# A fused attention and Mish block on one core: the weighted sums of two steps in one block, ScalarE's other work every second step

## The chip, the cores and the metric

The kernel runs on one core of one Trainium2 chip. The metric is the device time in microseconds, the median of several runs. A profile of one execution, taken by the hardware profiler, goes with it. The core's engines run side by side: TensorE (PE; its weight loads are listed as PEld), VectorE (DVE), ScalarE (ACT), GpSimd (POOL), and SyncE (SP), which issues the DMAs here. Results of matmuls land in PSUM, eight banks of 128 partitions by 512 words of 32 bits.

## What is computed

```python
x = A_x                                   # 1 x 2048 x 512
xn = _layernorm(x, axis=-1)
s = _A_ref(xn, A_wq, A_wk, A_wv, A_wo)    # attention, 32 query heads of 16, one k and v head
g = _silu(_B_ref(xn, B_w1, B_b1, B_w2))   # 512 -> 1792, Mish, 1792 -> 512
return x + s * g
```

In A, scores are q k / 4, softmax runs over all 2048 keys, and the heads' outputs are multiplied by wo. In B, the activation is h * tanh(softplus(h)).

## The kernel before

**The work in steps.** Queries are taken in NU = 32 units: 512 tokens (one of four token chunks) by four heads. Each unit goes through the 2048 keys in 16 steps of 128 keys, so there are NS = 512 steps; the main loop runs them in order at s = 0, 1, 2, ... A step holds four kinds of matmul on TensorE:

- **e** (e_one, L1098): four score matmuls of 64 contraction rows, 128 keys by 512 queries. ScalarE turns each into a pt tile with Exp (L1100). Even and odd steps use different halves of the array's rows; two steps together make two key blocks.
- **m** (m_one, L1119): score matmuls of a later unit, the other way round, of which VectorE takes the maximum (L1123); it is subtracted later. Mostly four a step.
- **xps**: a part of a "group", the other dense work (query projections, the two layers of the MLP, the wo product). A group has 12 or 15 matmuls in FP32R, high and low parts of each operand (mm12). Mm.half (L120) runs each as two halves of 64 rows, both into one PSUM bank.
- **pv** (pv, L1187): the weighted sums. For each key block, four matmuls with 128 rows and 32 output columns, one in each quarter of the columns; pt is FP32 here, and each stands as two instructions in the trace, so a step has eight. They accumulate over a unit's 16 steps in one bank.

e, m and xps use one half of the rows each, so two of them run at a time, one on each half; pv uses all rows.

**The banks.** Three for e, three for m, one for pv, one for xps.

**How a step is written down.** `waves(h, em, new)` issues the row matmuls of a step, h = s % 2. If no chunk is open it may take a new one, when `new` allows that and a group is ready: part of a group, mostly 6 of 12 matmuls, or 8 and then 7 of 15 (`chunk_size`). In this step it issues the chunk's first halves, in rows h, alternating with e and m matmuls on the other rows; in the next step the second halves, in the rows of the other h. Because both halves write one bank, the first matmul of a half is made to wait for a **relay**: the exponential or maximum of the e or m matmul that waves issued just behind the last xps matmul of the half before. The lines:

```python
i = xs.popleft().half(ps, h)
if first and cur["relay"] is not None:
    tc.add_manual_dep(i.ins, cur["relay"].ins.name, ...)
...
if len(a) > 1 or a and not xs:
    r = a.popleft()()
    if k and not xs and relay is None:
        relay = r
```

After the last chunk of a group, finish runs its `post`, which evacuates the bank with ScalarE or VectorE. `em` gives the order of e and m ("MEMEMEME"), m_sides how many m go on each half.

**The order around it.** After waves come `act_jobs` (ScalarE's other work: the Exp and Ln of the Mish, of the gate, and of the softmax sums, kept in the queue `jobs`, each of which starts the next piece of its own chain, on POOL too), `due` (what is timed for this step: DMAs and POOL work) and `pv_to(s - 2)`, which issues pv of the steps up to s - 2. When a unit's 16 are done, pv_to calls o_out: a copy of the bank on ScalarE (os), eight DMAs on SP, and later the two jobs of the softmax sums. `gap` counts evacuations on ScalarE, and act_jobs gives out less when there was one. Ready times and due times are kept in planned steps (STEP_US = 2.95), at build time; the order on every engine is fixed. The last LEAD = 20 steps (from s = 492) run two at a time through late_pair, with pv_to at every second one; a scheduled stage ahead of the loop does the loading, layernorm, keys and values and the first query projections.

Of the kernel before, what the change touches and what calls it, by code (L numbers as in the profile page):

```python
# [33 lines left out]
LEAD = 20  # L34
# [28 lines left out]
def m_need(v):  # L63

    return (34, 64)[v] if v < 2 else 32 * (v + 1)
# [61 lines left out]
def block_kernel(ctx: ExitStack, tc: tile.TileContext, x, wq, wk, wv, wo, w1, b1, w2, out):  # L127
# [275 lines left out]
    jobs = deque()  # L403
# [5 lines left out]
    gap = [0]  # L409
    ran = [0]  # L410

    def act_jobs(n):
        n = (int(len(jobs) > 3) if gap[0] else n) if n < 9 else n
        gap[0] = 0
        while n > 0:
            k = next((k for k, (fn, free) in enumerate(jobs)
                      if free is None or free() is not None and free() <= step[0]), None)
            if k is None:
                return
            fn = jobs[k][0]  # L420
            del jobs[k]
            fn()
            n -= 1
            ran[0] += 1
# [128 lines left out]
    def begin():  # L553
        prepare()
        if qqueue and is_ready(qqueue[0]):
            g = qqueue.popleft()
        elif queue and is_ready(queue[0]):
            g = queue.popleft()
        else:
            n = next((n for n, g in enumerate(queue) if g.wo is None), None)  # L560
            if not n or not is_ready(queue[n]) or queue[n].m1 is None:
                return False
            g = queue[n]
            del queue[n]
        if g.start:
            g.start()
        if len(g.mms) == 15 and spare_steps() > 1:
            g.most = 5
        if g.alloc:
            ps = g.alloc()  # L570
        else:
            ps = ps_x.tile([P, 512], F32, tag="x", name="xps")
        cur.update(g=g, n=0, ps=ps, chunk=[], relay=None)
        return True

    def finish():
        g = cur["g"]
        if cur["n"] < len(g.mms):
            return False
        for i in g.items:  # L580
            i.users -= 1
        cur["g"] = None
        evacs[0] += g.dve
        if lead:
            lead["post"](g, cur["ps"])
        else:
            g.post(cur["ps"])
            g.done = step[0]
        return True
# [98 lines left out]
    def chunk_size(n, most):  # L688
        return -(-n // -(-n // most)) if n else 0

    def waves(h, em, new):

        if not cur["chunk"] and (not new or cur["g"] is None and not begin()):
            mms = []
        else:
            g = cur["g"]
            mms = cur["chunk"] or g.mms[cur["n"]:cur["n"] + chunk_size(len(g.mms) - cur["n"], g.most)]  # L700
        second = bool(cur["chunk"])
        k = len(mms)
        ms = em(k, second)
        a = deque(ms[1 - h])
        b = deque(ms[h])
        ps = cur["ps"]
        ends = second and cur["n"] + k == len(cur["g"].mms)
        xs = deque(mms)
        swap = k % 2 and k > 5 and not second
        relay = None  # L710
        first = True
        done = False
        while a or b or xs:
            if xs:
                i = xs.popleft().half(ps, h)
                if first and cur["relay"] is not None:
                    tc.add_manual_dep(i.ins, cur["relay"].ins.name, mybir.DependencyInfo(
                        mybir.DependencyClass.Sync, mybir.DependencyReason.DATA), reason="other half of the bank")
                first = False
                if ends and cur["g"].dve and len(xs) == HOLD + k % 2:  # L720
                    held[0] = []
                if not xs and ends:
                    cur["n"] += k
                    cur["chunk"] = []
                    finish()
                    done = True
                    for top in held[0] or ():
                        top()
                    held[0] = None
            elif b and not swap:  # L730
                b.popleft()()
# [4 lines that stand above are left out]
            if b and swap and not xs and not a:  # L736
                b.popleft()()
        if k and not done:
            assert relay is not None
            cur["relay"] = relay  # L740
            if second:
                cur["n"] += k
                cur["chunk"] = []
            else:
                cur["chunk"] = mms
# [432 lines left out]
    def pv(s):  # L1178
        v, k = divmod(s, 16)
        if k == 0:  # L1180
            pv_of[v] = ps_v.tile([P, C], F32, tag="v", name=f"pv{v}")
        o = pv_of[v]
        for p in range(2):
            for a in range(2):
                pt = pt_of.pop((s, p, a))
                j = 2 * p + a
                pe.matmul(o[32 * j:32 * j + 32], vaug[:, k], pt, start=(k == 0), stop=(k == 15))  # L1187
# [83 lines left out]
    NS = 16 * NU  # L1271

    nc.scalar.preload_act_table_set("natural_log_exp_and_others")
    def due(t):
        step[0] = t
        for k in sorted(k for k in timed if k <= t):
            for fn in timed.pop(k):
                fn()
# [179 lines left out]
    while True:  # L1458
# [21 lines left out]
        s, e, k = min(opts, key=lambda o: o[0])  # L1480
# [36 lines left out]
        elif k == "J":  # L1517
            tag = next((g for g in ("wq", "ws", "wb") if (g == "wq" or s > 19.0) and arrived(g) and busy[0] + E0 < s + 0.5), None)
            n = ran[0]
# [26 lines left out]
    def pv_to(s):  # L1546

        while pv_next[0] <= s:
            k = pv_next[0]
            pv(k)  # L1550
            pv_next[0] += 1
            if k % 16 == 15:
                o_out(k // 16)
                return

    for s in range(NS + 2000):
        inm = s < NS - LEAD
        if inm or cur["chunk"]:
            assert s < NS
            due(s)  # L1560
            h = s % 2

            def em(k, second):
                n, rest = m_sides(1 - h, k, second) if inm else (0, 0)
                x = deque(lambda i=i: e_one(s, i) for i in range(4))
                y = deque(lambda: m_one(1 - h) for _ in range(n))
                r = [[], []]
                for op in EM if k % 2 == 0 or k == 5 or second else EM[::-1]:
                    if op == "M" and y:
                        r[1 - h].append(y.popleft())  # L1570
                    elif op == "E":
                        r[1 - h].append(x.popleft())
                r[h] = [lambda j=j: m_one(h, n + rest > 4 and j == rest - 1) for j in range(rest)]
                return r

            if s >= 2 and (s - 1) % 16 == 0 and s > 1:
                gap[0] += 1
            waves(h, em, s < NS - LEAD - 1)
            act_jobs(1 + (len(jobs) > 3))
            due(s + 0.5)  # L1580
            pv_to(s - 2)
        elif s < NS:
            due(s)
            if not late_banks:
                late_banks.extend(ps_m.tile([P, C], F32, tag="m", name=f"late{k}") for k in range(3))
                if (NS - s) % 2:
                    for i in range(4):
                        e_one(s, i)
                    fill(4)
                    act_jobs(1)  # L1590
                    pv_to(s - 2)
                    step[0] = s
                    continue
            if (NS - s) % 2 == 0:
                late_pair(s)
            else:
                if s < NS - 3:
                    act_jobs(1)
                pv_to(s - 1)
        else:  # L1600
            due(s)
            if s == NS:
                act_jobs(2)
                pv_to(NS - 1)
                due(s + 0.5)
                lanes_end()
                fill(3)
                fill(3)
            fill(16)
            act_jobs(100)  # L1610
        step[0] = s
        if vdone[0] < 8 * NC and min(m_next) >= m_need(vdone[0]):
            r = c_rows(vdone[0])
            rowq.extend([lambda r=r: (r[0](), behind.append(r[1])),
                         lambda r=r: (r[2](), behind.append(lambda: (r[3](), r[4]())))])
            vdone[0] += 1
        if rowq and not evacs[0]:
            rowq.popleft()()
        while behind and s >= NS - LEAD - 1:
            behind.popleft()()  # L1620
        evacs[0] = 0
        pump()
        if s > NS + 1 and not queue and cur["g"] is None and not timed and not jobs:
            break
# [12 lines left out]
```

## Time and profile before

| | |
|---|---|
| median of 3 runs | 1576.38 us (1576.18 to 1576.9) |
| the profiled execution | 1576.55 us |
| its span, first to last instruction | 1574.4 us |
| granted TensorE clock | 1.000 |
| instructions | 31742 |
| POOL busy | 633.7 us (40%) |
| DMA | 79 GB/s in the mean |

Times in the timeline are microseconds from the span's start. A row of the timeline gives start, duration, engine, line, operation, tiles (out<-in), shape and count; rows of one kind that follow each other are merged (x4, x8), and brackets tell how long the engine was idle before it and what released it. A row of a group gives the count, busy time and the mean of one in ns, then the idle time before and its releasers. A row of the waits: who, for whom, us in total, times, longest. A row of the stretches: the stretch and its length, the busy time of PE, PEld, DVE, ACT and POOL with instructions, then the clock and the DMA's share and rate.

### The profile page before, as it was taken

The page shows a single profiled execution, that of the slowest core. Times are in us where ns is not written, and L with a number is a line of the kernel's source. Part 1 is how long each engine was busy: PE and PEld are TensorE (multiplying, and loading weights), DVE is VectorE, ACT ScalarE, POOL GpSimd, SP SyncE. Part 2 cuts the span into 40 slices and gives each one's busy share as a digit, 9 for nine tenths or more (in the row PEclk, how much of TensorE's full clock was granted, in tenths as well). Part 3 has the DMA queues.
Part 4 walks back from the last instruction along what each step waited for, and adds up shares of the span by engine and source line. Part 5 has one row for each costly group of instructions (what it writes and reads, how often), then busy time and mean ns, then how long its engine had stood idle before and what let it go on. Part 6 is the DMA issues. An engine that isn't in the chain of part 4 may idle for free.

```text
span 1574.4 us, 31742 instructions
## 1 busy us (share of the span) xinstructions
PE 1562.6 (99%) x11738; PEld 842.0 (53%) x11738; DVE 1341.1 (85%) x2329; ACT 1307.8 (83%) x2518; POOL 633.7 (40%) x683
## 2 busy tenths in 40 slices
PE   9999999999999999999999999999999999999998
PEld 5555555555555555555555555555555555555554
DVE  8998888889889888888998988888889998888832
ACT  7588788798998779878989887887898878789886
POOL 4774266284464105503515320471251515126412
PEclk9999999999999999999999999999999999999999
DMA  6243231232331314122032222211332213032020
GB/s 191 93 124 112 65 101 44 60 118 84 125 97 41 103 44 137 45 69 83 24 100 65 64 93 69 85 59 30 112 99 85 74 40 111 19 111 58 15 81 28
DMA packets 74666, 124.31 MB, mean 79 GB/s; under 512 B 21520, under 2 KB 35344, under 8 KB 74512
## 3 DMA queue, kind: packets, MB, share of 16 engines
q1 hardware_dynamic: 74512, 122.29, 25.2%
q8 instruction: 93, 1.52, 0.4%
q14 instruction: 61, 0.50, 0.1%
HBM read 74.78 MB, written 26.21 MB: 64 GB/s over the span
## 4 chain that ended last, share of the span: by engine, by line
PE 95%; DVE 4%; ACT 1%; DMA 0%; issue 0%; SPq 0%; ACTq 0%; DVEq 0%
PE xps L120 44%; PE pv L1187 32%; PE e L1098 9%; PE m L1119 7%; DVE mb L1123 3%; PE late L120 1%; PE xps L116 0%; ACT pt L1100 0%; DMA xin<-in_dram 0%; PE late L1098 0%; PE kp L351 0%; PE wop L120 0%; PE xp L302 0%; PE late L116 0%; PE wop L116 0%
## 5 line engine op out<-in xcount | busy, mean ns | idle before, releaser
L1123 DVE TENSOR_REDUCE mb<-m 128x1 f32<-128x512 f32 x2048 | 1274.2, 683 | 171.3 <-PE m L1119 152.3
L1100 ACT ACTIVATE pt<-e 128x512 f32<-128x512 f32 x2018 | 1061.6, 602 | 220.7 <-PE e L1098 212.3
L1119 PE MATMUL m<-ks,qt 48*128 48x512 f32 (+1 forms) x2048 | 829.9, 421 | 1.6 <-DVE ks L239 0.5
L1098 PE MATMUL e<-qt,ks 64*128 64x512 f32 x2018 | 740.4, 401 | 0.3
L1187 PE MATMUL pv<-pt,vaug 128*32 128x512 f32 x4096 | 543.0, 604 | 0.0
L1119 PEld LDWEIGHTS m<-ks,qt 48*128 48x128 f32 (+1 forms) x2048 | 372.9, 185 | 55.7 <-DVE mb L1123 18.5
L1098 PEld LDWEIGHTS e<-qt,ks 64*128 64x128 f32 x2018 | 373.3, 186 | 17.9 <-ACT pt L1100 7.5
L120 PE MATMUL xps<-wbs,act 64*128 64x512 f32 x1248 | 339.1, 408 | 0.2
L120 PEld LDWEIGHTS xps<-wbs,act 64*128 64x128 f32 x1248 | 217.7, 185 | 177.4 <-ACT pt L1100 105.8
L120 PE MATMUL xps<-xt,ws 64*128 64x512 f32 x1104 | 305.8, 410 | 0.1
L120 PEld LDWEIGHTS xps<-xt,ws 64*128 64x128 f32 x1104 | 190.6, 185 | 182.7 <-ACT pt L1100 116.5
L174 POOL TENSOR_SCALAR t<-t 128x512 f32<-128x512 f32 x56 | 34.4, 615 | 395.1 <-ACT t L838 394.9
L1187 PEld LDWEIGHTS pv<-pt,vaug 128*32 128x32 f32 x4096 | 81.9, 108 | 137.4 <-issue 129.1
L164 POOL TENSOR_TENSOR hb<-hb,t 128x512 f32<-128x512 f32 x56 | 72.1, 1287 | 65.6 <-ACT t L851 52.4
L120 PE MATMUL xps<-xt,wq 64*128 64x512 f32 x336 | 93.2, 410 | 0.0
L120 PEld LDWEIGHTS xps<-xt,wq 64*128 64x128 f32 x336 | 58.0, 185 | 55.2 <-ACT pt L1100 35.2
L120 PE MATMUL xps<-wbs,ot_all 64*128 64x512 f32 x288 | 79.5, 409 | 0.0
L120 PEld LDWEIGHTS xps<-wbs,ot_all 64*128 64x128 f32 x288 | 49.6, 185 | 46.7 <-ACT pt L1100 29.3
L164 POOL TENSOR_TENSOR hb<-hb,u 128x512 f32<-128x512 f32 x56 | 72.3, 1291 | 4.4
L164 POOL TENSOR_TENSOR u<-u,t 128x512 f32<-128x512 f32 x56 | 71.8, 1282 | 4.7
L164 POOL TENSOR_TENSOR act<-hb,act 128x512 fp32r<-128x512 f32 x55 | 70.8, 1288 | 4.6
L159 POOL TENSOR_SCALAR qh<-qf 128x512 fp32r<-128x512 f32 x15 | 9.3, 620 | 111.8 <-ACT qf L770 76.2
(158 smaller groups left out, 954.9 us busy)
## 6 DMA issues: line engine op xcount, KB each, us to landing
wbs<-w SPq DMA_DIRECT2D x36, 512.0 KB
ws<-w SPq DMA_DIRECT2D x35, 512.0 KB
qt<-qh SPq DMA_DIRECT2D x256, 32.0 KB
w<-wbs SPq DMA_DIRECT2D x14, 512.0 KB
wq<-wq SPq DMA_DIRECT2D x14, 512.0 KB
wbs<-wo SPq DMA_DIRECT2D x12, 512.0 KB
rawws<-in_dram SPq DMA_DIRECT2D x21, 256.0 KB
rawwb<-in_dram SPq DMA_DIRECT2D x20, 256.0 KB
```

Source lines behind the costliest of these rows:

```text
L120: i = self.pe.matmul(ps, self.lhs()[o], self.rhs()[o], start=(self.k == 0 and self.halves == 0), stop=(self.k == self.tot - 1 and self.hal ...
L159: pool.tensor_scalar(o, i, 1.0, 0.0, op0=ALU.mult, op1=ALU.add)
L164: eng.tensor_tensor(out=o, in0=a, in1=b, op=op)
L174: pool.tensor_scalar(o, o, lim, 0.0, op0=ALU.min, op1=ALU.max)
L1098: pe.matmul(e, ks[o:o + 64, P * k:P * (k + 1)], q[o:o + 64, p], start=True, stop=True)
L1100: r = act.activation(pt, e, AF.Exp, scale=0.25)
L1119: pe.matmul(m, q[o, p, P * t:P * (t + 1)], ks[o, C * kb:C * (kb + 1)], start=True, stop=True)
L1123: r = dve.reduce_max(out=mb_of[v][:, kb, z:z + 1], in_=m, axis=AX.X)
L1187: pe.matmul(o[32 * j:32 * j + 32], vaug[:, k], pt, start=(k == 0), stop=(k == 15))
```

## The change

```diff
     def act_jobs(n):
-        n = (int(len(jobs) > 3) if gap[0] else n) if n < 9 else n
+        n = max(n - gap[0], int(len(jobs) > 3)) if n < 9 else n
         gap[0] = 0
...
             if s >= 2 and (s - 1) % 16 == 0 and s > 1:
                 gap[0] += 1
-            waves(h, em, s < NS - LEAD - 1)
-            act_jobs(1 + (len(jobs) > 3))
+            waves(h, em, s < NS - LEAD - 1 and s % 2)
+            if s % 2 == 0:
+                act_jobs(2 + (len(jobs) > 4))
             due(s + 0.5)
-            pv_to(s - 2)
+            if s % 2 == 0 or s == NS - LEAD - 1:
+                pv_to(s - 1)
```

Behind every even step pv_to issues the weighted sums of two steps, s - 2 and s - 1, one after the other: four groups of four, sixteen instructions. Odd steps have none (but the last one of the loop). waves may open a new chunk on odd steps alone, so first halves fall on odd steps and second halves on even ones. ScalarE's jobs are given out on even steps, two or three at a time, less one for each evacuation since the last time, and at least one while more than three wait.

## Prediction

> **What bounds the kernel now.** First the page: who is busy, and what the chain that ended last ran through.
>
> ```profile
> PE 1562.6 (99%) x11738; PEld 842.0 (53%) x11738; DVE 1341.1 (85%) x2329; ACT 1307.8 (83%) x2518; POOL 633.7 (40%) x683
> ...
> PE 95%; DVE 4%; ACT 1%; DMA 0%; issue 0%; SPq 0%; ACTq 0%; DVEq 0%
> ```
>
> TensorE is both. Then the table by stretches, to see which stage the change reaches:
>
> ```profile
> 87.26:1510.93 1423.67, 1422.79 (x10938) 763.50 (x10934) 1251.69 (x2123) 1201.63 (x2297) 568.06 (x573) 1.00 0.25 76
> ```
>
> These 1423.67 us are 490 steps of the main loop, 2.91 us each, with TensorE never idle. Over two steps VectorE works 1251.69/245 = 5.11 us of 5.81 and ScalarE 4.90: VectorE has 12% to spare. Now one step in the order of time (start, duration, engine, what):
>
> ```profile
> 802.68 1.07 PE L1187 MATMUL pv<-pt,vaug 128*32 128x512 f32 x8
> 803.68 0.50 PE L120 MATMUL xps<-xt,wq 64*128 64x512 f32 x1
> 803.68 0.50 PE L1119 MATMUL m<-ks,qt 48*128 48x512 f32 x1
> ...
> 804.02 0.40 PE L120 MATMUL xps<-xt,wq 64*128 64x512 f32 x1
> ...
> 804.25 2.48 DVE L1123 TENSOR_REDUCE mb<-m 128x1 f32<-128x512 f32 x4 [0.26 <-PE m L1119]
> ...
> 804.46 2.07 ACT L1100 ACTIVATE pt<-e 128x512 f32<-128x512 f32 x4 [0.28 <-PE e L1098]
> ...
> 804.95 0.39 PE L120 MATMUL xps<-xt,wq 64*128 64x512 f32 x1
> 804.96 0.39 PE L1098 MATMUL e<-qt,ks 64*128 64x512 f32 x1
> ...
> 805.19 0.42 PE L1098 MATMUL e<-qt,ks 64*128 64x512 f32 x1
> ...
> 805.54 1.06 PE L1187 MATMUL pv<-pt,vaug 128*32 128x512 f32 x8
> ...
> 806.38 0.65 ACT L913 ACTIVATE e<-y 128x512 f32<-128x512 f32 x1
> ...
> 808.38 1.07 PE L1187 MATMUL pv<-pt,vaug 128*32 128x512 f32 x8
> ```
>
> A step is the pv block (802.68 to 803.68, 1.00 us) and then the rows: seven pairs of matmuls on the two halves of the array, 803.68 to 805.54, 1.86 us. Two steps take 808.38 - 802.68 = 5.70 us. While the block runs, ScalarE and VectorE finish what the rows left in PSUM: the four exponentials run to 804.46 + 2.07 = 806.53, the four maxima to 806.73, both inside the block that began at 805.54. The block is TensorE's own work, but it is also the time in which the other two catch up.
>
> **What the change removes.** One pv block in two goes, and its eight matmuls are put behind the eight of the next. The tail of this same profile already has such blocks:
>
> ```profile
> 1516.62 1.92 PE L1187 MATMUL pv<-pt,vaug 128*32 128x512 f32 x16
> ...
> 1518.48 0.50 PE L1098 MATMUL e<-qt,ks 64*128 64x512 f32 x1
> ```
>
> Sixteen take 1.86 us from start to the first row matmul, two blocks of eight 2.00: 0.14 saved. The break in the rows goes too: the first pair after a block takes 804.02 - 803.68 = 0.34 and the last one before it 805.54 - 805.19 = 0.35, where a pair inside takes 0.23 (six starts from 804.02 to 805.19): 0.11 + 0.12. A merged pair of blocks is worth 0.37 us, 245 of them 90 us, if nothing else becomes late.
>
> **What it adds: a wait that the block hid.** A chunk of a group (xps) goes over two steps: in the first through one half of the array, in the second through the other, into the same PSUM bank. waves ties the first matmul of the second half to a relay: the exponential or maximum of the e or m matmul that was issued beside the last xps matmul of the first half. That gives a real wait, seen on the weight loads:
>
> ```profile
> PEld xps L120 <- ACT pt L1100: 301.6, 360, 1.0
> ...
> PEld m L1119 <- DVE mb L1123: 18.5, 56, 0.8
> ```
>
> 360 times 0.84 us: the length of a block, in which nothing is loaded for the rows. So before, the relay was ready within the block. After the change a chunk may only begin on an odd step, its second half comes on the even step, and the block stands behind the even step alone: **between the two halves there is no block any more.** All e and m matmuls of the even step are queued behind the waiting one on TensorE.
>
> When is the relay there? With six xps matmuls it is the third exponential: the sixth xps at 804.95 has the third e at 804.96 beside it. Its row:
>
> ```profile
> 805.43 0.60 ACT L1100 ACTIVATE pt<-e 128x512 f32<-128x512 f32 x1
> ```
>
> It ends at 806.03, 2.35 us after the rows began, while the rows alone would reach the second half after 1.86 - 0.35 + 0.23 = 1.74. What a relay costs beyond its end is seen in the tail, where a memset on VectorE is the relay between halves with no block between:
>
> ```profile
> 1530.07 0.09 DVE L638 MEMSET turns<- 128x1 f32 x2 [4.25 <-PE xps L120]
> 1530.21 0.18 PEld L120 LDWEIGHTS late<-xt,act 64*128 64x128 f32 x1 [0.19 <-DVE turns L638]
> ...
> 1530.29 0.43 PE L120 MATMUL xps<-xt,act 64*128 64x512 f32 x1
> ...
> 1530.56 0.39 PE L120 MATMUL xps<-xt,qt 64*128 64x512 f32 x1
> ```
>
> Relay ends 1530.16, matmul starts 0.13 later, the next pair 0.27 after it (0.07 less than after a block). So from the first matmul of the second half to the block: 1.86 - 0.07 = 1.79.
>
> The Trainium skill (TensorE: Matmul & The Clock Gate, "The mechanism" of Part 3) says that TensorE pulls a weight load ahead of matmuls in flight when it is for another row group. By it the weights would be there when the relay comes, and some 0.1 us of each restart, 25 us in all, would go. The row at 1530.21 speaks against it: there the load itself came 0.05 after the relay.
>
> Two steps with six xps matmuls: 2.35 + 0.13 + 1.79 + 1.86 = **6.13 us, against 5.70: 0.43 slower.** Chunks of eight and seven need rows of their own (TensorE, then ScalarE):
>
> ```profile
> 254.64 0.50 PE L120 MATMUL xps<-wbs,act 64*128 64x512 f32 x1
> ...
> 256.72 1.06 PE L1187 MATMUL pv<-pt,vaug 128*32 128x512 f32 x8
> 257.72 0.50 PE L120 MATMUL xps<-wbs,act 64*128 64x512 f32 x1
> ...
> 259.88 1.07 PE L1187 MATMUL pv<-pt,vaug 128*32 128x512 f32 x8
> ```
>
> ```profile
> 255.42 2.06 ACT L1100 ACTIVATE pt<-e 128x512 f32<-128x512 f32 x4 [0.49 <-PE e L1098]
> ...
> 258.26 2.11 ACT L1100 ACTIVATE pt<-e 128x512 f32<-128x512 f32 x4 [0.17 <-PE e L1098]
> ```
>
> Here the relay is the fourth exponential. Eight: it ends at 257.48, 2.84 after the rows' start at 254.64; rows 2.08, step 3.08. After: 2.84 + 0.13 + (2.08 - 0.07) + 1.86 = 6.84, against 6.16: 0.68 slower. Seven: relay at 260.37, 2.65 after 257.72; the second half is a step of seven pairs. After: 2.65 + 0.13 + 1.79 + 1.86 = 6.43, against 3.16 + 2.85 = 6.01: 0.42 slower.
>
> **How many of each.** From the groups by line (first those of xps):
>
> ```profile
> L1123 DVE TENSOR_REDUCE mb<-m 128x1 f32<-128x512 f32 x2048 | 1274.2, 683 | 171.3 <-PE m L1119 152.3 <-PE xps L120 15.6
> ...
> L120 PE MATMUL xps<-wbs,act 64*128 64x512 f32 x1248 | 339.1, 408 | 0.2
> L120 PE MATMUL xps<-xt,ws 64*128 64x512 f32 x1104 | 305.8, 410 | 0.1
> ...
> L120 PE MATMUL xps<-xt,wq 64*128 64x512 f32 x336 | 93.2, 410 | 0.0
> ...
> L120 PE MATMUL xps<-wbs,ot_all 64*128 64x512 f32 x288 | 79.5, 409 | 0.0
> ...
> L120 PE MATMUL xps<-xt,early 64*128 64x512 f32 x138 | 39.0, 411 | 0.2 <-ACT pt L1100 0.2
> ```
>
> A group of fifteen leaves 30 half matmuls, one of twelve 24. Of 1248, 32 groups of fifteen take 960 (thirds 0 and 1 of four token chunks); the rest, 288 + 1104 + 336 + 288 + 138 = 2154, are about 90 groups of twelve, 180 chunks of six. 245 chunks fill 490 steps, so some 60 are the eights and sevens, 30 each, and 5 are fives, which I price as six. Sum: 185 x 0.43 + 30 x 0.68 + 30 x 0.42 = 80 + 20 + 13 = **113 us** on the profiled 1576.55 (span 1574.4 and 2.15 around it; the median is 0.17 less): 1690.
>
> **The other edits.** VectorE's three m banks: the eighth m of two steps needs the fifth maximum done. Maxima begin 0.57 after the rows (804.25 - 803.68) and every (2.48 - 0.68)/3 = 0.60, so the fifth ends at 0.57 + 2.40 + 0.68 = 3.65 and the eighth m can go at 3.78. With the relay it is due at 2.48 + 1.44 = 3.92: hidden, and 0.3 us if the relay is not there (next part). ScalarE's jobs: 246 in all (three for each of 56 hidden blocks and 16 gates, two for 15 pairs of o), 0.65 each, before about one a step, now two behind every even step. Today a job starts 806.38 - 805.54 = 0.84 into the block; two then end at 0.84 + 1.30 = 2.14, before the next exponential at 1.86 + 0.78 = 2.64: cost nothing. With an evacuation and three jobs the exponentials could come late; my estimate for the bad end is one exponential's 0.60 in every fourth chunk, 37 us. The jobs' followers on POOL, and o_out's eight DMAs on SP (now one step sooner), have that slack: POOL is 40% busy. Its os copy had one step to free pv's one bank and has two now. A chunk that isn't ready on an odd step now loses two steps; by the count above hardly a step of the loop is without xps today, and a chunk left for the tail costs its twelve halves there, six pairs of 0.23 and a restart, about 2 us: nothing to 20 us for ten.
>
> **Rivals.** *Only the m banks bind* (the wait of the second half names an earlier exponential than I think): the eighth m at 3.78, + 0.35 + 1.86 = 5.99 for six, 0.29 over; for eights, with one more pair behind that m, 6.22, 0.06 over, and sevens taken alike. 185 x 0.29 + 60 x 0.06 = 57: 1634. For it: 56 waits on VectorE stand in the profile. Against it: waves' code makes the relay the op beside the last xps.
>
> *Faster: TensorE remains the bound*, and only the drain counts: 1576.5 - 90 = 1486. For it: 99% busy, and blocks of sixteen measured in the tail. It decides from the point where the relay ends under 2.35 - 0.43 = 1.92 us after the rows' start and the eighth m goes under 3.78 - 0.29 = 3.49. Against it: the third e alone ends at 805.35, 1.67 after the start, and its exponential takes 0.60. The Trainium skill (TensorEngine Tiling (Array Packing), "Key Properties") says that a change of tiling mode drains TensorE, and would have this rival win; the trace agrees on the drain, 0.37 us, and it is in the sum.
>
> *More is lost:* ScalarE late (37) and chunks missed (20) on top: 1690 + 57 = 1747.
>
> **How the numbers follow.** Relay as summed, with up to half of those additions and 30 less for restarts: 1660 to 1735, 74%. Banks alone, 1620 to 1660: 9%. More lost, over 1735: 9%. Faster: 7%, and 1% for no change. The range 1620 to 1740 leaves out the ends. A measurement of this kernel tells some 0.2% from no change. Faster 0.07, same 0.01, slower 0.92.
>
> **What would show it.** Right: pv blocks of sixteen, 1.86 us, and half as many; first xps of an even step 0.13 after the third exponential's end (fourth with seven or eight), TensorE idle before it some 0.7 to 1 us with ScalarE named; two steps of six in 6.1 us; TensorE's share near 90%. Wrong: even steps that begin 0.23 after the odd step's last pair (the faster rival), or the idle time in front of m with VectorE named (the banks), or exponentials that begin late behind jobs.

## The result and the profile after

The changed kernel takes 1699.55 us (median of 4 runs, 1698.02 to 1701.42), the kernel before 1576.45 (1576.18 to 1576.9): a ratio of 1.0781, 95% interval 1.0762 to 1.0800. The forecast was 1690, slower, within 1620 to 1740. The profiled execution took 1699.96 us, its span 1698.0.

The page of the changed kernel: engines, the chain that ended last, and the group of the pv matmuls.

```profile
PE 1558.2 (92%) x11738; PEld 885.9 (52%) x11738; DVE 1331.6 (78%) x2331; ACT 1312.2 (77%) x2518; POOL 633.6 (37%) x683
...
PE 69%; ACT 26%; DVE 3%; issue 1%; DMA 0%; SPq 0%; POOL 0%; ACTq 0%; DVEq 0%
PE xps L120 28%; PE pv L1187 27%; ACT pt L1100 25%; PE e L1098 6%; PE m L1119 5%; DVE mb L1123 2%; PE xps L116 0%; PE late L120 0%; ACT os L1196 0%; PE late L1098 0%; DMA xin<-in_dram 0%; ACT t L847 0%; PE kp L351 0%; PE wop L116 0%; PE xp L302 0%
...
L1187 PE MATMUL pv<-pt,vaug 128*32 128x512 f32 x4096 | 492.9, 599 | 0.0
```

Each engine did nearly the same work as before, and pv took less time for it (492.9 against 543.0). But the chain, 95% on TensorE before, now goes through the exponentials (ACT pt) for a quarter of the span. The waits say where it changes over:

```profile
PEld xps L120 <- ACT pt L1100: 282.2, 332, 1.2
...
PE xps L120 <- ACT pt L1100: 127.0, 242, 0.8
```

The first line, weight loads, is nearly what it was. The second is new: the matmuls of xps now wait too, 242 times, which is once in nearly every pair of steps. Two steps in the order of time show it:

```profile
864.08 1.92 PE L1187 MATMUL pv<-pt,vaug 128*32 128x512 f32 x16
...
865.93 0.49 PE L120 MATMUL xps<-xt,wq 64*128 64x512 f32 x1
...
866.47 4.94 DVE L1123 TENSOR_REDUCE mb<-m 128x1 f32<-128x512 f32 x8 [0.59 <-PE m L1119]
...
866.73 2.06 ACT L1100 ACTIVATE pt<-e 128x512 f32<-128x512 f32 x4 [0.36 <-PE e L1098]
...
867.20 0.39 PE L120 MATMUL xps<-xt,wq 64*128 64x512 f32 x1
867.21 0.39 PE L1098 MATMUL e<-qt,ks 64*128 64x512 f32 x1
...
867.44 0.44 PE L1098 MATMUL e<-qt,ks 64*128 64x512 f32 x1
868.35 0.18 PEld L120 LDWEIGHTS xps<-xt,wq 64*128 64x128 f32 x1 [0.79 <-ACT pt L1100]
868.35 0.50 PE L120 MATMUL xps<-xt,wq 64*128 64x512 f32 x1 [0.48 <-ACT pt L1100]
...
868.69 0.39 PE L120 MATMUL xps<-xt,wq 64*128 64x512 f32 x1
...
870.20 1.92 PE L1187 MATMUL pv<-pt,vaug 128*32 128x512 f32 x16
```

The block takes 1.85 us (864.08 to 865.93). The odd step's last pair starts at 867.44, and where the next pair would come at 867.67, TensorE stands until 868.35. In a narrower window the second and third exponential are

```profile
867.22 1.08 ACT L1100 ACTIVATE pt<-e 128x512 f32<-128x512 f32 x2
```

so the third ends at 868.30, and the weight load goes 0.05 later. Two steps take 870.20 - 864.08 = 6.12 us.

From the starts of the pv blocks, the distance of two successive ones by the number of row matmuls between them (28, 30 and 32 in two steps for chunks of six, seven and eight; in the kernel before, two steps in a row that hold such a chunk: 343, 29 and 30). Medians, in us; the last column is the median time. The rows below the second are experiments that follow: a later relay, an earlier one on VectorE (relay_dve), half maxima, and the last one, with three waits lifted:

| kernel | six (178) | seven (30) | eight (30) | time |
|---|---|---|---|---|
| before | 5.70 | 5.99 | 6.15 | 1576.4 |
| after | 6.14 | 6.46 | 6.83 | 1699.6 |
| relay_late | 6.63 | 7.08 | 6.83 | 1806.8 |
| relay_dve | 6.00 | 6.44 | 6.45 | 1663.3 |
| after_halfmax | 6.14 | 6.40 | 6.83 | 1693.2 |
| relay_dve_halfmax | 5.69 | 5.82 | 6.24 | 1568.1 |
| three_lifted | 5.64 | 5.78 | 6.24 | 1563.8 |

**The whole account.** From the block behind step 2 to that behind step 490: 86.26 to 1503.86 before, 87.59 to 1625.54 after, 120.35 us more. The rest of the 123.55 by which the span grew: 1.33 ahead of it (in this execution the granted clock stood at 0.50 from 81.7 to 88.5, in the one before at 1.00), 0.95 in step 491, which may not open a chunk but has a block of its own, and 0.92 in the tail.

### The profile page after: what moved, and what is told of

Same layout as the page of the kernel before. It is cut to its first block, busy times and chain, and to the rows that moved or that the text cites. A ratio compares the mean times of both kernels' runs of the same rounds, so it can differ in the third digit from the quotient of the medians.

```text
span 1698.0 us, 31802 instructions
## 1 busy us (share of the span) xinstructions
PE 1558.2 (92%) x11738; PEld 885.9 (52%) x11738; DVE 1331.6 (78%) x2331; ACT 1312.2 (77%) x2518; POOL 633.6 (37%) x683
## 4 chain that ended last, share of the span: by engine, by line
PE 69%; ACT 26%; DVE 3%; issue 1%; DMA 0%; SPq 0%; POOL 0%; ACTq 0%; DVEq 0%
PE xps L120 28%; PE pv L1187 27%; ACT pt L1100 25%; PE e L1098 6%; PE m L1119 5%; DVE mb L1123 2%; PE xps L116 0%; PE late L120 0%; ACT os L1196 0%; PE late L1098 0%; DMA xin<-in_dram 0%; ACT t L847 0%; PE kp L351 0%; PE wop L116 0%; PE xp L302 0%
## 5 line engine op out<-in xcount | busy, mean ns | idle before, releaser
L1187 PE MATMUL pv<-pt,vaug 128*32 128x512 f32 x4096 | 492.9, 599 | 0.0
L1119 PEld LDWEIGHTS m<-ks,qt 48*128 48x128 f32 (+1 forms) x2048 | 372.6, 185 | 58.3 <-DVE mb L1123 18.6
L1187 PEld LDWEIGHTS pv<-pt,vaug 128*32 128x32 f32 x4096 | 107.0, 109 | 222.3 <-issue 212.9
```

Of the source, the lines that this page charges most:

```text
L1119: pe.matmul(m, q[o, p, P * t:P * (t + 1)], ks[o, C * kb:C * (kb + 1)], start=True, stop=True)
```

## Experiments

All were timed beside the kernel before. "Relay theory" in what was expected is the prediction's account: the second half of a chunk waits for its relay, and no block hides that any more. The first three take the change apart.

**Only the chunk rule**

```diff
-            waves(h, em, s < NS - LEAD - 1)
+            waves(h, em, s < NS - LEAD - 1 and s % 2)
```

> Only the rule that a chunk opens on odd steps; a block of eight still stands behind every step, jobs as before. Relay theory: every relay is ready inside a block as before, so 1576 plus at most three chunks left for the tail: 1574 to 1584. Rival (chunks missed on even steps are the loss): over 1600.

1583.99 us, ratio 1.0050 (1.0033 to 1.0066). As the theory has it, at the upper edge of its range. In the profiled execution (1589.0; 4.6 us of it lie ahead of the loop, where the granted clock stood at 0.50 for 13.5 us) eleven steps had e and m alone, two before, and from step 491's block to the end of the span it took 76.1 us (1511.08 to 1587.2) against 67.5: what was missed was done in the tail, some four chunks at the prediction's 2 us each, where at most three were expected. The rule costs little while a block stands behind every step.

**Only the jobs**

```diff
-            act_jobs(1 + (len(jobs) > 3))
+            if s % 2 == 0:
+                act_jobs(2 + (len(jobs) > 4))
```

(with the new line in act_jobs)

> Only ScalarE's jobs given out on even steps, two or three at a time; blocks and chunks as before. Relay theory: two jobs end 2.1 us after a block of 1.0 begins, so the next step's first exponential is up to 0.36 late in the busiest stretches, the relay still within the next block: 1576 to 1600. Rival (bunching the jobs is what costs the 123 us): near 1690.

1597.19 us, ratio 1.0128 (1.0108 to 1.0148), inside the theory's range and far from the rival's. The 385 steps with fourteen row matmuls take 2.909 us in the mean, 2.859 before: 19 of the 21 us. Bunched jobs are too long for a block of eight.

**Only the merged blocks**

```diff
-            pv_to(s - 2)
+            if s % 2 == 0 or s == NS - LEAD - 1:
+                pv_to(s - 1)
```

> Only the weighted sums of two steps in one block on even steps; chunks may open on any step, jobs every step. Relay theory: where chunks open on odd steps the first to second half boundary has no block, where they open on even steps the second half to next first half boundary has none, and either waits for an exponential or an evacuation: the whole loss is there, and jobs between the steps add up to 0.2 per two steps: 1690 to 1740. Rival (the loss is in the chunk rule or the jobs, and merged blocks gain 90): near 1490.

1719.87 us, ratio 1.0904 (1.0882 to 1.0926). The merged blocks alone cost more than the whole change; the other two parts save 20 of it. With merged blocks and the chunk rule, but jobs every step:

> Merged blocks and the chunk rule, but ScalarE's jobs every step as before. Theory: a job behind the odd step's exponentials makes those of the even step 0.2 late in the two steps that have one there, so slower than the changed kernel by 5 to 25: 1705 to 1725, and near the kernel with merged blocks alone (1720). Rival (moving the jobs costs here what it costs alone, 21): 1680.

1713.58 us, ratio 1.0863 (1.0845 to 1.0881). So of those 20 the jobs' move makes about 14 by the medians, and 11 between two runs with the same granted clock, 0.998 (1710.38 and 1699.14): what costs 21 beside single blocks pays beside double ones. The rival fails.

**A later relay**, in the changed kernel:

```diff
-                if k and not xs and relay is None:
+                if k and not xs:
                     relay = r
```

> The changed kernel, but the relay is the last exponential or maximum that waves pops from the list beside the xps matmuls: with six xps the fourth exponential for the third (0.48 later), with seven a maximum about 0.6 later, with eight the same one. Relay theory: 185 x 0.48 + 30 x 0.6 = 107 more than the changed kernel, 1800 (1780 to 1820). Rival (the three m banks bind, relay hidden behind them): the changed kernel's time, 1700, to within 30.

1806.80 us, ratio 1.1459 (1.1432 to 1.1487), 107 above the changed kernel: the number of the relay theory. By class (table): six 0.49 more, one exponential's spacing; seven 0.62; eight, where the relay stays the same, nothing. Were the wait hidden behind another, this would have cost less or nothing. Its waits, the second those of the 30 sevens, whose relay is now a maximum:

```profile
PE xps L120 <- ACT pt L1100: 200.7, 213, 1.0
...
PE xps L120 <- DVE mb L1123: 34.2, 30, 1.2
```

**An earlier relay**, in the changed kernel, a memset on VectorE right behind the last xps matmul of a half:

```diff
+                if not ends and len(xs) == 1:
+                    held[0] = []
+                if not ends and not xs:
+                    relay = dve.memset(turns[:, 0:1], 0.0)
+                    tc.add_manual_dep(relay.ins, i.ins.name, SYNC, reason="half of the bank")
+                    for top in held[0] or ():
+                        top()
+                    held[0] = None
```

> The changed kernel with an earlier relay: a memset of one column on VectorE right behind the last xps matmul of a half, put ahead of the maximum of the m matmul beside the last but one. It ends 1.85 us after the rows begin with six xps (third exponential: 2.35). Relay theory with the banks behind it: with six the eighth m now waits for the fifth maximum (3.73 + 0.13), 6.07 against 6.13 measured; with eight 6.45 against 6.83; with seven about 6.2 against 6.45: 183 x 0.06 + 30 x 0.38 + 30 x 0.25 = 30 off, 1670 (1650 to 1690). Banks alone without relay in the changed kernel: no change, 1700. Relay alone without banks: 1700 - 185 x 0.5 - 60 x 0.5 = 1580 or less.

1663.33 us, ratio 1.0550 (1.0534 to 1.0566), 36 off the changed kernel, 30 expected. The split differs: six gain 0.14 (0.06 expected), eight 0.38 (as expected), seven 0.02 (0.25 expected). The rows of two steps with six, a slow pair (6.27, the median is 6.00), in which small reductions stand among VectorE's maxima, and this kernel's wait for the m banks:

```profile
803.23 0.50 PE L120 MATMUL xps<-wbs,act 64*128 64x512 f32 x1
...
805.01 0.06 DVE L723 MEMSET turns<- 128x1 f32 x1
...
805.14 0.50 PE L120 MATMUL xps<-wbs,act 64*128 64x512 f32 x1
...
807.22 0.50 PE L1127 MATMUL m<-ks,qt 48*128 48x512 f32 x1 [0.16 <-DVE mb L1131]
...
807.65 1.92 PE L1195 MATMUL pv<-pt,vaug 128*32 128x512 f32 x16
```

```profile
PEld m L1127 <- DVE mb L1131: 117.8, 420, 1.0
```

The second half begins 1.91 after the rows, 0.51 sooner than with the third exponential. But then TensorE waits for maxima to free the m banks, 117.8 us in all, 18.6 in the changed kernel. By the medians, the second half of the sixes begins 0.49 sooner and takes 0.36 longer to the block, that of the sevens 0.55 sooner and 0.52 longer: this is where the sevens' gain went. The wait that was taken away uncovers the next one.

**Half maxima**, in the changed kernel, in the one with the early relay, and in the kernel before:

```diff
-            r = dve.reduce_max(out=mb_of[v][:, kb, z:z + 1], in_=m, axis=AX.X)
+            r = dve.reduce_max(out=mb_of[v][:, kb, z:z + 1], in_=m[:, 0:C // 2], axis=AX.X)
...
-        r = act.activation(pt, e, AF.Exp, scale=0.25)
+        r = act.activation(pt, e, AF.Exp, scale=0.015625)
```

> The changed kernel with the maxima taken over half of the columns, which leaves half of that work out (and a smaller scale in the exponentials, to keep them finite): VectorE's maxima are shorter, the three m banks come free sooner, the relay stays the third exponential. Relay theory: the banks cost only where the small reductions of a unit's maxima delay them, so 1685 to 1700. Banks alone: 1700 - 120 - 90, near 1490.

1693.18 us, ratio 1.0739 (1.0721 to 1.0757), as the relay theory has it: with the relay in place, shorter maxima on VectorE hardly count.

> The kernel before with half of the maxima's columns left out: both theories say TensorE bounds it and VectorE is hidden, so 1570 to 1577. If VectorE already bounded the kernel before, 1550 or less, and the comparison of the two kernels with half maxima would have to be made against that.

1570.88 us, ratio 0.9967 (0.9954 to 0.9980). TensorE bounds the kernel before: the loop's steps are the same (2.850 in the median), and 4.6 of the 5.6 us lie ahead of the loop (first block at 81.67, 86.26 before), where maxima run too; so do 4.2 of the 6.4 by which half maxima shorten the changed kernel (first block at 83.40, 87.59 without). This is what the next two kernels are to be compared with.

> Both at once: early relay and half maxima (half of the maxima's columns left out). If the relay and the banks are the two waits that stand between the changed kernel and the saving of 0.37 per merged block: six 5.5 to 5.6, eight 6.17, seven 5.7: 1530 to 1555, faster than the kernel before. If a third thing costs (blocks of sixteen, jobs): over 1600.

1568.12 us, ratio 0.9948 (0.9933 to 0.9963): a miss. Half maxima take 95 us off the kernel with the early relay and 6 off the changed kernel, so the wait for the m banks is real once the relay is gone. It is nearly away here:

```profile
PEld m L1127 <- DVE mb L1131: 12.9, 32, 0.8
```

With both waits lifted the two kernels are nearly equal, 1568 and 1571, and the saving of 0.37 for each merged block is still not there. Two steps with six (rows from 796.16):

```profile
796.16 0.50 PE L120 MATMUL xps<-xt,wq 64*128 64x512 f32 x1
...
796.97 4.03 ACT L1108 ACTIVATE pt<-e 128x512 f32<-128x512 f32 x8 [0.41 <-PE e L1106]
...
798.00 0.49 PE L120 MATMUL xps<-xt,wq 64*128 64x512 f32 x1
...
799.57 0.49 PE L1106 MATMUL e<-qt,ks 64*128 64x512 f32 x1
...
799.99 1.92 PE L1195 MATMUL pv<-pt,vaug 128*32 128x512 f32 x16
```

The second half is in time (1.84), but the exponentials run without a break, and the last e goes at 799.57: the fifth ends at about 796.97 + 4 x 0.49 + 0.60 = 799.53. With three banks for e that one has to wait for it. So the last experiment put the eighth e of two steps into the ring of the m banks:

```diff
-ps_e.tile([P, C], F32, tag="e", ...)
+(ps_m if s < NS - LEAD and s % 2 == 0 and i == 3 else ps_e).tile(..., tag="m" if ... else "e", ...)
```

> Early relay and half maxima (half of the maxima's columns left out, as before), and the eighth e matmul of two steps in the m ring of banks, so that it need not wait for the fifth exponential. In the kernel with early relay and half maxima alone, two steps with six xps took 5.69: second half at 1.84, and 1.99 instead of 1.85 from there to the block, with the last e 0.04 behind the fifth exponential's end. Theory (the third wait is the e banks): 1.84 + 1.85 + 1.86 = 5.55 with six, so 178 x 0.14 = 25 off 1568, 1543 (1535 to 1555). Rival (what is left is the restart behind the relay or the block itself): 1563 to 1573.

1563.80 us, ratio 0.9920 (0.9905 to 0.9935): another miss, at the edge of the rival's range. The e banks were worth 0.05 of the 0.14 in the median of the sixes and 0.01 in their mean: the 47 in which small reductions of a unit's maxima stand on VectorE got 0.08 slower (5.73 and 5.81), and the other 131 got 0.04 faster (5.69 and 5.64, all four means). The rows of a pair of the median length show the rest:

```profile
793.77 0.50 PE L120 MATMUL xps<-xt,wq 64*128 64x512 f32 x1
...
795.04 0.39 PE L120 MATMUL xps<-xt,wq 64*128 64x512 f32 x1
...
795.50 0.06 DVE L723 MEMSET turns<- 128x1 f32 x1
...
795.62 0.50 PE L120 MATMUL xps<-xt,wq 64*128 64x512 f32 x1
...
795.96 0.39 PE L120 MATMUL xps<-xt,wq 64*128 64x512 f32 x1
...
797.13 0.49 PE L1106 MATMUL e<-qt,ks 64*128 64x512 f32 x1
797.56 1.92 PE L1195 MATMUL pv<-pt,vaug 128*32 128x512 f32 x16
```

The second half starts 1.85 after the first where 1.74 is a step without a break: 0.11. Its first pair takes 0.34, not 0.23: 0.11. The last pair takes 0.43 to the block, not 0.35: 0.08. Together 0.30 of the 0.37; the rest, 0.07, is about what two steps gain (5.64 against 5.70). The boundary between two halves breaks the rows as the block did, even with the earliest relay: the last xps matmul of the first half ends at 795.43, and its partner in the same bank can go at 795.62.

## Why the prediction was right

- **What a merged block saves**: sixteen in 1.86 foretold from the tail, 1.85 measured. The other part of the 0.37, the break in the rows, came back at the boundary between the two halves.
- **The relay**: foretold 0.13 behind the third exponential and 0.27 to the next pair; measured 0.05 (in each of the 178) and 0.34 (0.33 to 0.37). Both sizes were off, by about as much in opposite directions, so the sum came out right, 0.40 foretold and 0.39 measured: that part is luck. The end of the exponential, which is most of it, was read rightly (2.35 foretold, 2.37 in the pair above). Two steps with six came out at 6.14 for 6.13, with seven at 6.46 for 6.43, with eight at 6.83 for 6.84. That it is this wait is shown by the later relay, dose by dose.
- **The counts**: 185, 30 and 30 foretold from the halves by tile; 178, 30 and 30 in the 244 pairs of the account above, and six pairs with fewer xps or none.
- **The rule on weight loads** of the Trainium skill (TensorE: Matmul & The Clock Gate, "The mechanism" of Part 3): the load behind the relay was not pulled ahead of it here; load and matmul stand at 868.35 together, 0.05 after the exponential.
- **The m banks**: foretold to be hidden behind the relay. Shown by half maxima (6.4 us less, 4.2 of them ahead of the loop) and by the early relay, which uncovers them.
- **The jobs**: foretold to cost nothing beside double blocks; their move saves 11 to 14 there and costs 21 beside single ones.
- **What was too small**: the sum, 113 against 120 in the loop. By the classes' means (5.72, 6.01 and 6.17 before; 6.19, 6.46 and 6.83 after) the sixes cost 84 us for 80, the sevens 14 for 13 and the eights 20 for 20; the rest lies in the six other pairs. The sixes' mean is 6.19, their median 6.14. The 47 of them in which the small reductions of a unit's maxima stand on VectorE take 6.31 in the mean, the other 131 take 6.15: 47 x 0.16 = 7.5 us. The prediction had allowed for late exponentials and missed chunks and not for this. It is not the m banks, since with half maxima the 47 take 6.30. In one of them (373.91 to 380.20) the second half begins on time, but the m beside it loads 0.18 later than the xps:

```profile
378.17 0.18 PEld L120 LDWEIGHTS xps<-xt,wq 64*128 64x128 f32 x1 [0.79 <-ACT pt L1100]
...
378.35 0.18 PEld L1119 LDWEIGHTS m<-ks,qt 48*128 48x128 f32 x1
```

In other two-step pairs both load together (at 868.35 above, to within 0.01). In the trace, wait instructions of their own stand in front of this m (the view of its line counts 250 such instructions, 0.05 each). All of the 47 have two of them there and a lag of the m behind the xps of over 0.1; none of the other 131 has either. That they are the 0.16, standing behind the waiting xps and so no longer done ahead, fits; no run took them out.

- **The range**: 1735, the top of the relay's part of it, does not follow from its words: half of the 57 of additions on top of 1690 is 1718. The measured 1699.55 lies under that too.
- **The faster rival** needed both waits gone; with both gone, at the price of half the maxima, it still would have been wrong, by the 0.30 above. Its 1486 counted the break at the block and not the one that the two halves of a bank make: a first pair takes 0.34 behind a relay as behind a block. What merged blocks are worth where no bank is handed over between the two steps was not run.

## What to carry to other kernels

Time in which the bottleneck does work that nobody waits for may be the cover of other engines' latency: before such work is moved, list each wait that ends within it, and ask what ends it when the cover is gone. Here a transition worth 0.37 us hid a wait of 0.7, and under that lay two more, for m banks and, a small one, for e banks. A wait's place in a profile ("xps waits for pt, 0.84 each") says that it exists and not whether it binds; how far its releaser is from the point where the work could have gone does.

## What the hardware showed unexpectedly

A hand-over between two row halves that write one bank, by way of another engine, costs much even when that engine is free. In the last experiment's rows it is 0.07 from the matmul's end (which the profile models) to the memset, 0.06 of memset, 0.06 to the next matmul, and then a first pair of 0.34 for 0.23. Beside that, in the changed kernel no weight load issued behind a matmul that waited for its relay went ahead of it: in all 178 pairs with six the partner's load, for the other half of the rows, came with it or up to 0.34 later, and never before.
